# The start and the output stores of a three-stage fp32 kernel: w_out loads behind the last y store, unit 0 in the output banks, six output buffers

## The chip, the cores and the metric

One core of a Trainium2 chip runs the whole program. The metric is the device time of one execution in microseconds (us); 1 KB is 1024 bytes here. Engines are named as in the profile: PE (matmul), PEld (its weight loads), DVE, ACT, POOL, and SP, whose queue issues every DMA of this kernel.

## The reference, cut to what is computed

```python
x   = attn(q, k, v)            # 4 batches x 8 heads x 576 positions x 64: banded + pooled softmax
x   = x.transpose(0, 2, 1, 3).reshape(2304, 512)
a   = x @ w1; b = x @ w2       # 512 -> 1024
y   = (a * b @ w3) @ w_out     # 1024 -> 1024 -> 512
h   = y @ w_in                 # 512 -> 2048          (moe2)
out = (h * sigmoid(h)) @ w_out # 2048 -> 512, [2304, 512] fp32
```

## The kernel before

Every product is built from two fp32r parts of each operand (a high part and the remainder) in three passes, `PASSES`, so a result tile takes three matmuls for each 128 rows of the contraction.

**Stage one** (to about 454 us of the span) is attention, the first products (`ab_group`, tiles `ab`) and, for half a batch at a time, `y_group`: tile `y` is summed in a PSUM bank, ACT copies it to one of two `yo` buffers, and an SP DMA stores it to the DRAM tensor `ydram`. Weights of the last stage are decoded on the way and stored to the DRAM tensors `wsd` (w_in) and `wod` (w_out).

**The last stage** computes moe2 from `ydram`. Tokens are taken in three groups `t` of 768 and w_in in eight parts `p`; a **unit** `u = 8t + p` is one of the 24 combinations. `h_unit(u)` makes seven products `h_0` to `h_6` (six matmuls of 128x384 each, one round of a two-by-two block scheme that saves one product in eight). ACT copies `h_0` to `p1` (tile `p`), DVE combines each later product with what it has (tiles `u2`, `u4`, `u3`) into `cf` (ready after `h_4`) and `cg` (ready after `h_6`). `silu` then runs a sigmoid on ACT (tile `sg`), a multiplication on DVE, a cast on DVE to the high part of `g`, and a subtraction on POOL for the low part of `g`; the last three are `rest()`. `after(k, fn)` puts `fn` behind the k-th next product.

The outputs of a unit are summed one unit later: `out_block` adds three matmuls of 128x512 to one of six banks `o_0` to `o_5`; `run_out(2)` after each product but the first runs two of them. So a unit on PE is: `h_0`, `h_1`, two blocks, `h_2`, two blocks, and so on to `h_6`. Unit 0 has no blocks to run. After the last part of a token group the six sums are copied (ACT and DVE in turn) to a ring of `os` buffers and stored to `out`, two DMAs each.

**Banks.** PSUM has eight banks: a ring of two, `S` (`s_tile`), which the products `h` share; two `T`, which hold `o_0` and `o_1`; four `mm`, which hold `o_2` to `o_5` and, in stage one, `ab` and `y`. A product waits until the bank of the product two before it has been read.

**DMA.** `wc_load(u + 2)` at the end of `h_unit(u)` loads a unit's w_in parts, `wca` (768 KB) and `wcb` (1024 KB), from `wsd` into buffers that unit u frees. `wo_load(p)` loads 1024 KB of w_out (`wo`) from `wod`; `wo_load(0)` stands ahead of the stage, `wo_load(u + 1)` at the start of `h_unit(u)` for u below 7. `y_load(t)` loads `yr` (two DMAs of 768 KB) from `ydram`; POOL then makes four differences (`y_mix`, tile `t`, in units 2 to 5 of a group), ACT and DVE or POOL split them into `yc`.

**Order.** In the last stage PE, DVE, ACT and POOL run in source order (`manual_schedule`). SP isn't in that list: a scheduler puts its DMAs where it takes them to be ready. On each queue an instruction that waits holds all behind it.

Of the kernel before, what the change touches and what calls it, by code (L numbers as in the profile page):

```python
# [8 lines left out]
F32 = mybir.dt.float32  # L9
# [5 lines left out]
NB, NHP, S, P = 4, 4, 576, 128  # L15
# [20 lines left out]
def tile_model(ctx: ExitStack, tc: tile.TileContext, qk, vw, vr, w12, w3t, wo, wb, out):  # L36
    nc = tc.nc
    wide = wo.dtype != F32

    def pool(stack, name, side, space=None, bufs=1):  # L40
        kw = {} if space is None else {"space": space}
        return stack.enter_context(
            tc.tile_pool(name=name, bufs=bufs, side=side, reuse_waits="tile", **kw)
        )
# [11 lines left out]
    ydram = tc.dram_tile([4, P, NTOK], F32, name="ydram")  # L56
# [3 lines left out]
    def mm_tile(name):  # L60
        return ps.tile([P, 512], F32, tag="mm", name=name, bufs=4)
# [4 lines left out]
    def s_tile(name):  # L66
        return ps.tile([P, 512], F32, tag="S", name=name, bufs=2)
# [461 lines left out]
    def mark(ins):  # L529
        anchor[ins.ins.engine] = ins.ins  # L530
# [38 lines left out]
        C[b, h, m] = c  # L569

    y_ps = {}

    def y_group(b, h, ec, part):
        N = TOK[h]
        if part == 0:
            y_ps[ec] = mm_tile(f"y{b}_{h}_{ec}")
        acc = y_ps[ec]
        for kf in range(4 * part, 4 * part + 4):
            c = C[b, h, kf]
            for n, (i, j) in enumerate(PASSES):  # L580
                nc.tensor.matmul(  # L581
                    acc[:, :N], lhsT=WP[kf // 2][:, i, kf % 2, ec * P:(ec + 1) * P],
                    rhs=c[:, j, :],
                    start=(kf == 0 and n == 0), stop=(kf == 7 and n == 2),
                )
            if ec == 3:
                C.pop((b, h, kf))
        if part == 1:
            yo = cpool.tile([P, TOK[0]], F32, tag="yo", name=f"yo{b}_{h}_{ec}")[:, :N]
            mark(nc.scalar.copy(yo, acc[:, :N]))  # L590
            t0 = b * S + OFF[h]
            nc.sync.dma_start(ydram[ec, :, t0:t0 + N], yo)

    slots, kinds = [], []

# [15 lines left out]
    for part in range(2):  # L611
        for ec in range(4):
            slots.append(lambda ec=ec, part=part: y_group(NB - 1, 1, ec, part))
            kinds.append(None)
# [147 lines left out]
    def y_high(t, i):  # L762
        name = CH[i][0]
        d = yp[0].tile([P, 2, 2, NH], F32R, tag="c_" + name, name=f"yc{t}_{i}")
        nc.scalar.copy(d[:, 0], Y[t][name])
        YC[t, i] = d

    def y_rest(t, i, alone=False):
        d = YC[t, i]
        e = nc.vector if i % 2 or alone else nc.gpsimd  # L770
        e.tensor_tensor(
            out=d[:, 1], in0=Y[t][CH[i][0]], in1=d[:, 0].bitcast(F32), op=ALU.subtract
        )
# [15 lines left out]
    def wo_load(p):  # L789
        t = wpool.tile([P, 2, 2, 512], F32R, tag="wA" if p < 4 else "wC", name=f"wo{p}")  # L790
        nc.sync.dma_start(t.rearrange("p l f n -> p (l f n)").bitcast(F32), wod[p])
        WO[p] = t
# [47 lines left out]
    s_c.close()  # L840
    s_x.close()
    b2 = pool(ctx, "b2", "right", bufs=2)
    wo_load(0)

    todo = []

# [2 lines left out]
    def out_block(u, half, j):  # L849
        t, p = divmod(u, 8)  # L850
        if p == 0 and half == 0:
            OUT[t, j] = ps.tile(
                [P, 512], F32, tag="T" if j < 2 else "mm", name=f"o{t}_{j}",
                bufs=2 if j < 2 else 4,
            )
        acc = OUT[t, j]
        g, w = G[u, half], WO[p]
        for n, (a, b) in enumerate(PASSES):
            nc.tensor.matmul(  # L859
                acc, lhsT=g[:, a, j * P:(j + 1) * P], rhs=w[:, b, half, :],  # L860
                start=(p == 0 and half == 0 and n == 0), stop=(p == 7 and half == 1 and n == 2),
            )
        if p == 7 and half == 1:
            if t < NT - 1:
                o = b2.tile([P, 512], F32, tag="o", name=f"os{t}_{j}", bufs=3)
            else:
                if not last:
                    last.append(yp[0].tile([P, 6, 512], F32, tag="raw", name="last"))
                o = last[0][:, j]
            if j % 2:  # L870
                nc.vector.tensor_copy(o, acc)
            else:
                nc.scalar.copy(o, acc)
            for k in range(2):
                r0 = 64 * ORDER[(t * 2 * NH + j * P) // 64 + k]
                nc.sync.dma_start(out[r0:r0 + 64, :], o[64 * k:64 * k + 64, :])

    def run_out(n):
        for _ in range(min(n, len(todo))):
            out_block(*todo.pop(0))  # L880

    def temp(tag, u, bufs=1, width=NH):
        return b2.tile([P, width], F32, tag=tag, name=f"{tag}{u}", bufs=bufs)
# [4 lines left out]
    def after(k, fn):  # L888
        later.setdefault(n_chain[0] + k, []).append(fn)

    def next_chain():
        n_chain[0] += 1
        for fn in later.pop(n_chain[0], []):
            fn()

    def silu(u, half, c):
        sg = temp("sg", f"{u}_{half}", 2, 2 * NH)
        nc.scalar.activation(sg, c, AF.Sigmoid)  # L898
        g = b2.tile([P, 2, 2 * NH], F32R, tag="g", name=f"g{u}_{half}", bufs=5)
        G[u, half] = g  # L900

        def rest():
            nc.vector.tensor_tensor(out=sg, in0=c, in1=sg, op=ALU.mult)
            nc.vector.tensor_copy(g[:, 0], sg)  # L904
            e = nc.vector if u == NUN - 1 else nc.gpsimd
            e.tensor_tensor(  # L906
                out=g[:, 1], in0=sg, in1=g[:, 0].bitcast(F32), op=ALU.subtract
            )

        if half == 0 and u:  # L910
            rest()
        else:
            after(2 - half, rest)

    def h_unit(u):
        t, p = divmod(u, 8)
        wc = WC.pop(u)
        k = {}
        if u < 7:
            wo_load(u + 1)  # L920

        def tt(out_, in0, in1, op=ALU.add):
            nc.vector.tensor_tensor(out=out_, in0=in0, in1=in1, op=op)  # L923

        cf = temp("c", f"f{u}", 2, 2 * NH)
        cg = None
        for i, (name, w, c) in enumerate(CH):
            acc_full = s_tile(f"h{u}_{i}")
            acc = acc_full[:, :NH]
            y = YC[t, i]  # L930
            n = 0
            for kt in range(2):
                for (a, b) in PASSES:
                    nc.tensor.matmul(  # L934
                        acc, lhsT=wc[w][:, a, c, kt * P:(kt + 1) * P], rhs=y[:, b, kt, :],
                        start=(n == 0), stop=(n == 5),
                    )
                    n += 1
            if i == 0:
                k["p1"] = temp("p1", u)  # L940
                nc.scalar.copy(k["p1"], acc)  # L941
            elif i == 1:
                tt(cf[:, :NH], acc, k["p1"])
            elif i == 2:
                k["u2"] = temp("u2", u)
                tt(k["u2"], acc, k["p1"])
            elif i == 3:
                k["u4"] = temp("u4", u)
                tt(k["u4"], acc, k["u2"])
            elif i == 4:  # L950
                tt(cf[:, NH:], acc, k["u4"])
            elif i == 5:
                cg = temp("c", f"g{u}", 2, 2 * NH)
                k["u3"] = temp("u3", u)
                tt(k["u3"], acc, k["u2"])
                tt(cg[:, NH:], acc, k["u4"])
            else:
                tt(cg[:, :NH], k["u3"], acc, ALU.subtract)
            next_chain()
            if i == 4:  # L960
                silu(u, 0, cf)
            elif i == 6:
                silu(u, 1, cg)
            if p == 7 and t + 1 < NT:
                after(1, lambda i=i: y_high(t + 1, i))
                after(3, lambda i=i: y_rest(t + 1, i))
            if 2 <= p < 6 and i == 5 and t + 1 < NT:
                y_mix(t + 1, p - 2)
            run_out(2 if i else 0)
        wc_load(u + 2)  # L970
        if p == 1 and t + 1 < NT:
            y_load(t + 1)

    E = mybir.EngineType
    with tc.manual_schedule(engines={E.PE, E.DVE, E.Activation, E.Pool}):
        for u in range(NUN):
            h_unit(u)
            assert not todo
            todo.extend((u, half, j) for half in range(2) for j in range(6))
        for _ in range(3):  # L980
            next_chain()
        assert not later
        run_out(12)
# [56 lines left out]
```

## Time and profile before

| | |
|---|---|
| time, median of 3 runs | 884.74 us (883.40 to 886.43) |
| the profiled execution | 884.52 us, its span 882.7 us |
| PE busy | 846.1 us, 96% of the span |
| DVE, ACT, POOL busy | 533.8, 300.5, 277.5 us |
| mean granted TensorE clock | 0.988 of full speed |
| DMA over the span | 149.17 MB, mean 169 GB/s |

The span runs from the first to the last instruction; the time of an execution is 1.8 us longer. The ends of matmuls are modelled, so neighbouring PE rows can overlap by some tenths of a microsecond.

### The profile page before, as it was taken

Reading aid. Unit: us, or ns where it says so; the run is one execution under the profiler, and the core shown is the slowest. Engines: PE = TensorE matmul, PEld = TensorE weight load, DVE = VectorE, ACT = ScalarE, POOL = GpSimd, SP = SyncE. Lnnn points to the kernel's source line nnn. Section 1 sums busy time; section 2 is a strip of 40 time slices with the busy share of each in tenths; the row PEclk is TensorE's granted clock in tenths of the full one; section 3 lists DMA queues with packets and bytes.
Section 4 is the critical chain, followed back from the end, with each engine's and each line's share of the span. In section 5 each row is a group of like instructions: output and inputs, shape, how many; then the busy total and the mean of one; then the engine's idle time right before and its main releaser. Section 6 shows DMA issues by size and latency. Waiting matters only on the chain.

```text
span 882.7 us, 17438 instructions
## 1 busy us (share of the span) xinstructions
PE 846.1 (96%) x7104; PEld 745.7 (84%) x7104; DVE 533.8 (60%) x857; ACT 300.5 (34%) x866; POOL 277.5 (31%) x220
## 2 busy tenths in 40 slices
PE   3999999999999999999999799999999999999996
PEld 2544598999999999999999698989889899899995
DVE  5899989577475848447955334445544446543434
ACT  5665755454454544433322101114111122211101
POOL 2000154344442535231325123325323235221220
PEclk9999998999999999999999899999999999999999
DMA  9945735464545463406984824324743252642403
GB/s 325 341 136 164 236 121 186 145 238 162 181 164 197 158 213 114 169 27 236 336 337 183 337 91 124 127 85 166 212 135 129 84 167 84 182 140 85 164 3 72
DMA packets 39729, 149.17 MB, mean 169 GB/s; under 512 B 4448, under 2 KB 11616, under 8 KB 33504
## 3 DMA queue, kind: packets, MB, share of 16 engines
q1 hardware_dynamic: 39648, 148.05, 49.3%
q8 instruction: 56, 0.92, 0.4%
q14 instruction: 25, 0.20, 0.1%
HBM read 115.52 MB, written 32.51 MB: 168 GB/s over the span
## 4 chain that ended last, share of the span: by engine, by line
PE 83%; DVE 8%; DMA 3%; ACT 2%; issue 2%; SPq 0%; POOL 0%; ACTq 0%; DVEq 0%
PE o L859 21%; PE ab L541 20%; PE h L934 19%; PE y L581 10%; PE wp L451 5%; PE ol L371 2%; PE sd L279 2%; DMA ydram<-yo 2%; PE tl L347 2%; PE s L328 1%; PE od L313 1%; DMA out<-os 1%; PE td L296 1%; DVE dec L175 1%; DMA lent<-wo 1%
## 5 line engine op out<-in xcount | busy, mean ns | idle before, releaser
L859 PE MATMUL o<-wo,g 128*128 128x512 f32 x864 | 221.7, 393 | 2.0 <-POOL g L906 2.0
L859 PEld LDWEIGHTS o<-wo,g 128*128 128x128 f32 x864 | 160.6, 188 | 27.5 <-POOL g L906 2.3
L906 POOL TENSOR_TENSOR g<-sg,g 128x768 fp32r<-128x768 f32 x46 | 85.5, 1859 | 259.0 <-DVE g L904 249.7
L934 PE MATMUL h<-yc,wcb 128*128 128x384 f32 x576 | 119.0, 343 | 5.8 <-ACT p L941 5.8
L934 PEld LDWEIGHTS h<-yc,wcb 128*128 128x128 f32 x576 | 105.5, 192 | 14.6 <-ACT p L941 6.9
L541 PE MATMUL ab<-x,w_wB 128*128 128x320 f32 (+1 forms) x768 | 111.0, 299 | 0.6 <-DVE cf L555 0.6
L541 PE MATMUL ab<-x,w_wA 128*128 128x320 f32 (+1 forms) x768 | 108.9, 299 | 0.6 <-DVE w_wA L192 0.6
L581 PE MATMUL y<-c,w_wC 128*128 128x320 f32 (+1 forms) x768 | 109.3, 298 | 0.0
L541 PEld LDWEIGHTS ab<-x,w_wB 128*128 128x128 f32 x768 | 103.8, 190 | 2.1 <-issue 1.0
L541 PEld LDWEIGHTS ab<-x,w_wA 128*128 128x128 f32 x768 | 103.6, 191 | 1.9 <-DVE w_wA L192 0.9
L566 POOL TENSOR_TENSOR c<-cf,c 128x320 fp32r<-128x320 f32 (+1 forms) x64 | 72.1, 1127 | 101.0 <-DVE c L565 77.7
L581 PEld LDWEIGHTS y<-c,w_wC 128*128 128x128 f32 x768 | 102.6, 188 | 1.2 <-issue 1.0
L898 ACT ACTIVATE sg<-cf 128x768 f32<-128x768 f32 x24 | 20.3, 847 | 186.9 <-DVE cf L923 186.9
L934 PE MATMUL h<-yc,wca 128*128 128x384 f32 x432 | 83.4, 336 | 0.1
L934 PEld LDWEIGHTS h<-yc,wca 128*128 128x128 f32 x432 | 76.5, 188 | 4.2 <-DVE cg L923 0.4
L451 PE MATMUL wp<-w_wo,w_w 128*128 128x512 f32 x128 | 61.9, 629 | 1.3 <-DVE w_w L179 1.2
L238 POOL TENSOR_TENSOR vr<-vr 72x512 f32<-72x512 f32 x12 | 19.2, 1596 | 120.8 <-DMA vr<-vr 120.8
L555 DVE TENSOR_TENSOR cf<-ab,af 128x320 f32<-128x320 f32 (+1 forms) x64 | 28.8, 451 | 45.9 <-PE ab L541 36.5
L923 DVE TENSOR_TENSOR u<-h,u 128x384 f32<-128x384 f32 x48 | 26.6, 554 | 39.8 <-PE h L934 39.6
L898 ACT ACTIVATE sg<-cg 128x768 f32<-128x768 f32 x24 | 20.3, 847 | 87.7 <-DVE cg L923 87.7
L252 ACT ACTIVATE band<-band,sm 128x38 f32<-128x38 f32 x144 | 44.9, 316 | 8.4 <-DVE sm L248 7.4
L451 PEld LDWEIGHTS wp<-w_wo,w_w 128*128 128x128 f32 x128 | 24.2, 199 | 27.9 <-issue 24.1
(120 smaller groups left out, 1060.6 us busy)
## 6 DMA issues: line engine op xcount, KB each, us to landing
wcb<-wsd SPq DMA_DIRECT2D x24, 1024.0 KB
wca<-wsd SPq DMA_DIRECT2D x24, 768.0 KB
sw<-wb SPq DMA_DIRECT2D x32, 512.0 KB
qk<-qk SPq DMA_DIRECT2D x16, 579.0 KB
wsd<-res SPq DMA_DIRECT2D x8, 1024.0 KB
wod<-res SPq DMA_DIRECT2D x8, 1024.0 KB
wo<-wod SPq DMA_DIRECT2D x8, 1024.0 KB
st<-w SPq DMA_DIRECT2D x14, 512.0 KB
```

The source lines that it names most:

```text
L238: side().tensor_tensor(out=r[:, :, 0:2, :], in0=r[:, :, 0:2, :], in1=r[:, :, 2:4, :], op=ALU.add)
L252: nc.scalar.activation(E[:, j, :], src[:, j, :], AF.Exp, bias=nb[:, j:j + 1], scale=scale, accum_out=sv[:, j:j + 1],)
L451: nc.tensor.matmul(acc, lhsT=w3v[:, k, j * P:(j + 1) * P], rhs=wov[:, k, :], start=(gp == 0 and k == 0), stop=(gp == 3 and k == 1),)
L541: nc.tensor.matmul(acc[:, :N], lhsT=wv[:, i, w, kk, :], rhs=x[:, j, :], start=(n == 0), stop=(n == 11),)
L555: nc.vector.tensor_tensor(out=cf, in0=acc[:, :N], in1=C.pop("af"), op=ALU.mult)
L566: mark(nc.gpsimd.tensor_tensor(out=c[:, 1], in0=cf, in1=c[:, 0].bitcast(F32), op=ALU.subtract))
L581: nc.tensor.matmul(acc[:, :N], lhsT=WP[kf // 2][:, i, kf % 2, ec * P:(ec + 1) * P], rhs=c[:, j, :], start=(kf == 0 and n == 0), stop=(kf = ...
L859: nc.tensor.matmul(acc, lhsT=g[:, a, j * P:(j + 1) * P], rhs=w[:, b, half, :], start=(p == 0 and half == 0 and n == 0), stop=(p == 7 and h ...
L898: nc.scalar.activation(sg, c, AF.Sigmoid)
L906: e.tensor_tensor(out=g[:, 1], in0=sg, in1=g[:, 0].bitcast(F32), op=ALU.subtract)
L923: nc.vector.tensor_tensor(out=out_, in0=in0, in1=in1, op=op)
L934: nc.tensor.matmul(acc, lhsT=wc[w][:, a, c, kt * P:(kt + 1) * P], rhs=y[:, b, kt, :], start=(n == 0), stop=(n == 5),)
```

## The change

Five edits. `wo_load(0)` is recorded with `tc.issue_after` of the last y store, so its DMA stands behind that store in the program; unit 0 puts its first six products into the banks of the outputs (`mm` for `h_0` to `h_3`, `T` for `h_4` and `h_5`, `S` for `h_6`); unit 0's first `rest()` runs at once instead of two products later (for all other units nothing moves: `after(1, rest)` is what the second half had); the `os` ring has six buffers instead of three; and SP joins the engines that run in source order.

```diff
-            nc.sync.dma_start(ydram[ec, :, t0:t0 + N], yo)
+            last_y[:] = [nc.sync.dma_start(ydram[ec, :, t0:t0 + N], yo)]
...
-    wo_load(0)
+    with tc.issue_after(last_y[0].ins):
+        wo_load(0)
...
-                o = b2.tile([P, 512], F32, tag="o", name=f"os{t}_{j}", bufs=3)
+                o = b2.tile([P, 512], F32, tag="o", name=f"os{t}_{j}", bufs=6)
...
-        if half == 0 and u:
+        if half == 0:
             rest()
         else:
-            after(2 - half, rest)
+            after(1, rest)
...
-            acc_full = s_tile(f"h{u}_{i}")
+            bank = s_tile if u or i == 6 else mm_tile if i < 4 else t_tile
+            acc_full = bank(f"h{u}_{i}")
...
-    with tc.manual_schedule(engines={E.PE, E.DVE, E.Activation, E.Pool}):
+    with tc.manual_schedule(engines={E.PE, E.DVE, E.Activation, E.Pool, E.SP}):
```

On PE, where the last stage begins, the rows of before are these (`yc` the split inputs, the name in brackets whose signal a row waits for):

```order
L934 MATMUL h_2_6456<-yc_2_6157,wcb_5883 128x384 [waits DMAHW6_49,Activation_49]
L934 MATMUL h_2_6456<-yc_2_6157,wcb_5883 128x384 x5
L934 MATMUL h_3_6465<-yc_3_6111,wcb_5883 128x384 [waits DVE_49]
L934 MATMUL h_3_6465<-yc_3_6111,wcb_5883 128x384 x5
L934 MATMUL h_4_6474<-yc_4_6176,wcb_5883 128x384 [waits DVE_49]
...
L934 MATMUL h_0_6517<-yc_0_6077,wca_5903 128x384 [waits DMAHW0_49,DVE_49]
```

And of the changed kernel:

```order
L937 MATMUL h_2_6456<-yc_2_6157,wcb_5883 128x384 [waits DMAHW6_49,Activation_49]
L937 MATMUL h_2_6456<-yc_2_6157,wcb_5883 128x384 x5
L937 MATMUL h_3_6465<-yc_3_6111,wcb_5883 128x384 [waits Activation_49]
L937 MATMUL h_3_6465<-yc_3_6111,wcb_5883 128x384 x5
L937 MATMUL h_4_6474<-yc_4_6176,wcb_5883 128x384 [waits PE_49]
...
L937 MATMUL h_0_6517<-yc_0_6077,wca_5903 128x384 [waits DMAHW0_49]
L937 MATMUL h_0_6517<-yc_0_6077,wca_5903 128x384 x5
L937 MATMUL h_1_6529<-yc_1_6093,wca_5903 128x384 [waits DVE_49]
```

The products stand in the same order. In unit 0 the waits for DVE are gone; `h_0` to `h_3` wait for ACT, which must have copied the `y` tiles out of the same four banks. The first wait for DVE is now that of unit 1's `h_1`, whose bank is that of unit 0's `h_6`.

On SP, around the last y stores, before:

```order
L744 DMA yr_6637<-ydram 128x4x384
L791 DMA wo_6436<-wod 128x2048
L791 DMA wo_6514<-wod 128x2048
L744 DMA yr_6637<-ydram 128x4x384
L791 DMA wo_6640<-wod 128x2048
L592 DMA ydram<-yo_1_0_6378 128x256
L791 DMA wo_6759<-wod 128x2048
L592 DMA ydram<-yo_1_1_6393 128x256
L592 DMA ydram<-yo_1_2_6408 128x256
L791 DMA wo_6878<-wod 128x2048
L592 DMA ydram<-yo_1_3_6423 128x256
L791 DMA wo_6996<-wod 128x2048
```

And of the changed kernel:

```order
L593 DMA ydram<-yo_1_0_6378 128x256
L593 DMA ydram<-yo_1_1_6393 128x256
L593 DMA ydram<-yo_1_2_6408 128x256
L593 DMA ydram<-yo_1_3_6423 128x256
L792 DMA wo_6432<-wod 128x2048
L792 DMA wo_6436<-wod 128x2048
L782 DMA wca_6510<-wsd 128x1536
L785 DMA wcb_6511<-wsd 128x2048
L792 DMA wo_6514<-wod 128x2048
L782 DMA wca_6633<-wsd 128x1536
L785 DMA wcb_6634<-wsd 128x2048
L745 DMA yr_6637<-ydram 128x4x384 x2
```

No load of w_out is left ahead of the y stores. The first stands right behind the fourth store, the others one to a unit between the w_in loads, and the `yr` loads of the second token group have moved from ahead of the y stores to behind unit 3's w_in loads.

On SP, at the first output stores, before:

```order
L781 DMA wca_7359<-wsd 128x1536
L784 DMA wcb_7360<-wsd 128x2048
L744 DMA yr_7628<-ydram 128x4x384 x2
L876 DMA out<-os_0_7442 64x512 x2
L781 DMA wca_7503<-wsd 128x1536
L876 DMA out<-os_1_7449 64x512 x2
```

And of the changed kernel:

```order
L782 DMA wca_7359<-wsd 128x1536
L785 DMA wcb_7360<-wsd 128x2048
L878 DMA out<-os_0_7442 64x512 x2
L878 DMA out<-os_1_7449 64x512 x2
L878 DMA out<-os_2_7467 64x512 x2
L878 DMA out<-os_3_7474 64x512 x2
L878 DMA out<-os_4_7492 64x512 x2
L878 DMA out<-os_5_7499 64x512 x2
L782 DMA wca_7503<-wsd 128x1536
```

The w_in load that stood between the first and the second store now stands behind all twelve, and the `yr` loads of the third group stand two units later.

## Rows read from the trace of the kernel before

**Rows 1.** Windows: stretch, length, busy PE PEld DVE ACT POOL, clock, DMA share, GB/s.

```profile
488.00:510.00 22.00, 15.78 (x71) 14.39 (x70) 9.16 (x13) 3.30 (x6) 4.28 (x2) 0.84 0.79 300
520.00:614.00 94.00, 94.00 (x470) 84.78 (x469) 43.17 (x68) 17.80 (x25) 32.02 (x18) 1.00 0.36 119
```

**Rows 2.** Chain that ended last, 483 to 512 us: start, length, what.

```profile
485.51 7.75 DMA ydram<-yo
...
494.16 6.91 PE h L934 x24
...
508.16 1.07 PE h L934 x6
509.23 1.37 PE o L859 x6
```

**Rows 3.** Timeline, 455 to 515 us: start, length, engine, operation, idle before it.

```profile
476.79 0.52 SPq L791 DMA_DIRECT2D wo<-wod  x1
...
484.10 0.32 SPq L592 DMA_DIRECT2D ydram<-yo  x1
...
487.74 2.25 PE L934 MATMUL h<-yc,wca 128*128 128x384 f32 x12
490.53 0.37 ACT L590 COPY yo<-y 128x256 f32<-128x256 f32 x1 [5.05 <-DMA ydram<-yo]
...
493.63 0.48 ACT L941 COPY p<-h 128x384 f32<-128x384 f32 x1
...
494.14 0.56 DVE L923 TENSOR_TENSOR cf<-h,p 128x384 f32<-128x384 f32 x1 [16.32 <-ACT p L941]
...
504.23 2.45 POOL L906 TENSOR_TENSOR g<-sg,g 128x768 fp32r<-128x768 f32 x1 [25.53 <-DVE g L904]
```

**Rows 4.** Windows of four microseconds after PE's first idle time, columns as in rows 1.

```profile
492.00:496.00 4.00, 1.84 (x6) 1.84 (x7) 0.56 (x1) 0.75 (x2) 0.00 (x0) 0.59 0.89 310
496.00:500.00 4.00, 4.00 (x15) 4.00 (x14) 1.12 (x2) 0.00 (x0) 0.00 (x0) 0.56 1.01 423
...
504.00:508.00 4.00, 2.03 (x11) 1.44 (x10) 3.53 (x4) 0.06 (x1) 3.21 (x2) 1.00 0.77 298
```

**Rows 5.** Chain, last stage: the first two products of units 7, 8, 10, 16, 18.

```profile
598.67 2.08 PE h L934 x12
...
614.33 2.09 PE h L934 x12
...
646.58 2.09 PE h L934 x12
...
740.54 2.09 PE h L934 x12
...
773.02 2.08 PE h L934 x12
```

**Rows 6.** Timeline, 598 to 645 us, around the first output stores.

```profile
624.41 0.85 ACT L898 ACTIVATE sg<-cf 128x768 f32<-128x768 f32 x1 [7.73 <-DVE cf L923]
...
625.29 0.96 DVE L903 TENSOR_TENSOR sg<-cf,sg 128x768 f32<-128x768 f32 x1 [0.97 <-ACT sg L898]
625.75 1.22 SPq L876 DMA_DIRECT2D out<-os  x2
...
626.28 0.56 DVE L904 CAST g<-sg 128x768 fp32r<-128x768 f32 x1
...
629.40 0.69 DVE L871 COPY os<-o 128x512 f32<-128x512 f32 x1 [1.03 <-PE o L859]
...
633.11 0.59 ACT L873 COPY os<-o 128x512 f32<-128x512 f32 x1 [1.61 <-DMA out<-os]
```

**Rows 7.** Timeline, yr's loads of group 0, and the first differences of groups 0, 1.

```profile
454.44 0.97 SPq L744 DMA_DIRECT2D yr<-ydram  x2
...
463.39 2.45 POOL L760 TENSOR_TENSOR t<-yr 128x768 f32<-128x768 f32 x1 [7.64 <-DMA ydram<-yo]
...
534.77 1.85 POOL L760 TENSOR_TENSOR t<-yr 128x768 f32<-128x768 f32 x1
```

More of the change, by code (lines that the diff above doesn't have):

```diff
@@ L571, in tile_model @@
     y_ps = {}
+    last_y = []
     def y_group(b, h, ec, part):
```

## Prediction

> **What bounds the kernel now.** I read the windows by stage first. Between 520 and 614 us PE is busy for all 94.00 us while POOL has 32 and DVE 43 [rows 1]: there PE is the bound, and nothing is won by making another engine quicker. The one long stretch that differs is the start of the last stage, 488 to 510 us, where PE is busy for 15.78 of 22 us at a granted clock of 0.84 [rows 1]. The chain says what ended last there: a y store, 485.51 to 493.26 us, then 24 matmuls that take 6.91 us [rows 2]. The timeline shows how a store comes to hold PE. Loads of w_out are issued until 477.3 us; the first of the last four y stores is issued at 484.10, and the copy that needs its buffer back runs at 490.53, after 5.05 us of waiting for it. ACT is in order, so the copy of h_0 runs at 493.63, though h_0 and h_1 began at 487.74 and took 2.25 us; DVE, which needs that copy, starts at 494.14, and only then does a bank of the ring of two come free [rows 3]. PE, idle since 490, gets a low clock as well: 0.59 and 0.56 of full speed from 492 to 500 us, about the 1.2 GHz level, and 1.00 (2.4 GHz) later [rows 4].
>
> The second thing to see is the rhythm. Units 7 and 8 begin 15.66 us apart; from unit 8 to unit 10 it is 32.25 us, and from 16 to 18 it is 32.48, where two units of 15.66 would be 31.32 [rows 5]. These are the two places where outputs are stored: a DVE copy waits until 629.40 and an ACT copy until 633.11, the latter for a store out of the ring of three [rows 6]. So what can be won is at most the start plus 0.93 and 1.16 us.
>
> **Start of the stage, rebuilt for the changed kernel.** I take unit 1's h_2 as the mark; it stands at 508.16 in the chain [rows 2]. A product takes half of the 2.09 us of a pair, 1.045 [rows 5], and is readable some 0.17 us after the next could start (487.74 + 2.25 against 487.74 + 2.09) [rows 3, 5].
>
> The banks: h_0 to h_3 need the four copies of y. The y products end at the latest when h_0 starts, 487.74. The copies take 0.37 each [rows 3]. How long an undisturbed y store takes no row shows. Above, it is the 6.4 us from 484.10 to 490.53, with three megabytes of w_out and more ahead of it; below, nothing. The nearest row is the output store issued at 625.75 whose buffer is written again at 629.40 [rows 6], at most 3.65 us. I take 3.65: then the third copy runs at 487.8 and the fourth, whose store left at 485.5, at 489.2, the copy of h_0 ends at 490.0 and nothing waits, since h_3 isn't due before 490.9.
>
> PE then runs all seven products and unit 1's h_0 without a stop, to 487.74 + 8 x 1.045 = 496.1. Meanwhile h_4 is readable at 493.1; DVE combines it (0.56 [rows 3]) until 493.7; sigmoid 0.85, multiplication 0.96, cast 0.56 [rows 6], 496.2 with the gaps between them. This is the third edit: the multiplication and cast now stand ahead of DVE's last three combinations. They cost 1.5 us there, since those combinations, 0.55 each, end at 497.85 instead of about 496.3, and unit 1's h_1 needs the bank that the last of them frees. So PE idles for 1.75 us. What the early rest() buys is the low part of g: POOL, 2.45 us [rows 3], ends at 498.7. h_1 runs from 497.9, the two blocks follow at 498.95 (the second matmul, at 499.2, is the first to need the low part), take 1.37 [rows 2], and h_2 starts at 500.3. That is **7.8 us** earlier than 508.16. Bounds: with no idle at all 487.74 + 9 x 1.045 + 1.37 = 498.5, a gain of 9.6; the lower bounds are rivals below.
>
> What covers it: the blocks need the first load of w_out, which now leaves SP only behind the fourth y store, about 489.5. Two yr loads issued from 454.44, with megabytes ahead of them, had landed by 463.39, 8.95 us later [rows 7]; so long a time for 1024 KB in an almost empty queue would be 498.4, still before 498.95. It is hidden, by little in the worst case.
>
> **The other loads of w_out**, seven of 1024 KB, go from one burst to one per unit, between the w_in loads. A unit then moves 1024 + 768 + 1024 KB, 2.9 MB in 15.66 us or 184 GB/s, against 300 that were moved in the window at the start [rows 1]. Each is used more than a unit after it is issued. I cost them at nothing.
>
> **yr in source order.** The loads of groups 1 and 2 now stand behind two w_in loads that wait for PE; they are issued about 0.7 us before a unit that begins at T, with 1.8 MB ahead of their own 1.6. At 300 GB/s that is 11 us, T + 11. POOL's first difference runs at 534.77, which is T + 14.4 for unit 2 (598.67 less five units is 520.37) [rows 5, 7]. Hidden, by 3 us.
>
> **Output stores.** With six buffers no copy waits for a store: os_3 moves from 629.40 to about 628.4, os_4 from 633.11 to about 630.5, h_0's copy follows at 631.1, and PE's next h_2 isn't due before 633.3. The two transitions give back **0.93 + 1.16** us [rows 5]. Bounds: nothing (if the copies themselves, and not their buffers, hold ACT and DVE up), and all of it. I take all, as by these times each copy ends two microseconds before PE wants what stands behind it. The w_in load that now follows twelve stores leaves at about 634 instead of 627 and is needed at 645.
>
> **Sum.** 884.52 (profiled execution) - 7.8 - 0.93 - 1.16 = 874.6; the median of the runs is 0.22 above that execution, so **874.8 us**, 1.1% faster. With the bounds 9.6 and 7.0 for the start and 2.1 and 1 for the stores its own range is 873 to 877.
>
> **Rivals.**
> - *The clock falls anyway.* The 1.75 us of idle before unit 1's h_1 could pull PE to half speed. Against it: after the idle time of 4 us around 492 the clock was 0.59, but from 504 to 508, with PE busy for 2.03 of 4 us, it stayed at 1.00 [rows 4]. Eight microseconds at 0.56 to 0.59 would lose some 3.4: 878.2. Chance 0.09. (The Trainium skill, TensorE: Matmul & The Clock Gate, section on a second HAM failure mode, speaks for this rival: short idle times between groups of matmuls that cycle through PSUM banks can be enough for the clock to swing. The row above, of 2 us idle and full clock, does not show it.)
> - *Output stores give nothing back,* because copies and not buffers hold the ring: 876.9. Chance 0.05.
> - *The y stores are slow by themselves,* 6.4 us without any load ahead. Then h_0's copy stays at 493.6. The new banks let PE run to 496.1 all the same, but DVE's chain starts at 494.1, unit 1's h_1 at 500.4, h_2 at 502.8, and after 4.3 us of idle the low clock costs its 2.7 us (6.91 for what takes 4.18 [rows 2, 5]): a gain of 2.6, and 880.0 with the stores. Chance 0.04.
> - *It doesn't do what it says: PE waits for w_out instead.* If the first load landed at 508.7, the start gives nothing and 882.7 remains, no measurable change. That needs 19 us for one megabyte; 8.95 for more than two [rows 7] speaks against. Chance 0.04.
> - *Slower: the yr loads are late.* SP holds them behind waiting loads. POOL's difference may start up to about T + 21.3 without harm: behind it stand a difference and a low part of g, 1.85 each (the difference is in [rows 7]; the subtraction for g takes 1.85 too outside the start), which PE wants at T + 15.66 + 9.4. Beyond, each microsecond is one for PE, in groups 1 and 2. The gain is gone when they land at T + 26.2, it is slower by over 0.3% beyond T + 27.6; T + 28 would give 888.2. Estimated landing is T + 11. Chance 0.04.
>
> **How the numbers follow.** The forecast has the remaining 0.74. A change of 0.3% (2.7 us) is about what a measurement of this kernel can tell from none. Faster by more: forecast and the first three rivals, 0.92; within it: the fourth, 0.04; slower: the fifth, 0.04. The range 872.5 to 878.6 takes in the forecast with its bounds and the first two rivals.
>
> **What would show it.** Right: ACT copies h_0 before 490.1; no PE idle time over 0.5 us between the last y product and unit 1's h_1, then about 1.75 us released by DVE; clock 1.00 from 488 on; unit 1's h_2 near 500.3; units 8 to 10 and 16 to 18 at 31.3 us; no ACT or DVE copy released by an output store. Wrong: PE waiting for a wo load or for POOL at the first block; POOL's difference in units 2 or 10 released by a DMA; a granted clock near 0.6 after 496; the copies of y still released by their stores.

## The result and the profile after

The changed kernel takes 874.14 us (median of 4 runs, 871.77 to 874.99) against 884.07 for the kernel before (4 runs): an estimated ratio of 0.9877, 95% interval 0.9854 to 0.9901 (the two medians alone give 0.9888). The prediction was 874.8, in a range of 872.5 to 878.6. The medians differ by 9.93 us; the sum of the prediction was 9.89. The interval stands for 8.8 to 12.9 us, so the rows below are the sharper check.

Below, **M** is the start of unit 1's `h_2` in the chain less the start of unit 0's `h_0` in the timeline: 508.16 - 487.74 = 20.42 us before [rows 2, 3].

The windows of the changed kernel, columns as in rows 1:

```profile
488.00:492.00 4.00, 4.00 (x25) 4.00 (x24) 1.88 (x4) 0.85 (x1) 0.00 (x0) 1.00 0.99 406
492.00:496.00 4.00, 2.61 (x16) 2.29 (x15) 3.05 (x6) 1.21 (x2) 1.81 (x1) 1.00 0.93 354
496.00:500.00 4.00, 4.00 (x21) 3.49 (x20) 2.20 (x4) 0.00 (x0) 1.83 (x1) 1.00 0.97 375
...
488.00:510.00 22.00, 20.61 (x107) 18.76 (x106) 11.36 (x20) 3.75 (x5) 5.49 (x3) 1.00 0.72 261
520.00:614.00 94.00, 94.00 (x470) 84.77 (x469) 48.85 (x69) 18.53 (x26) 38.08 (x20) 1.00 0.46 163
```

PE is busy for 20.61 of the 22 us from 488 to 510 instead of 15.78, and the clock stays at 1.00 where it was 0.84, with 0.59 and 0.56 in its low part [rows 1, 4]. One idle time is left, between 492 and 496. From 520 to 614 PE was the bound and still is.

The timeline at the start of the last stage, with the engine's idle time and its releaser in brackets:

```profile
481.04 0.37 ACT L591 COPY yo<-y 128x256 f32<-128x256 f32 x1 [7.79 <-PE y L582]
482.40 0.37 ACT L591 COPY yo<-y 128x256 f32<-128x256 f32 x1 [0.99 <-PE y L582]
483.80 0.37 ACT L591 COPY yo<-y 128x256 f32<-128x256 f32 x1 [1.03 <-PE y L582]
484.92 2.25 PE L937 MATMUL h<-yc,wca 128*128 128x384 f32 x12
485.16 0.37 ACT L591 COPY yo<-y 128x256 f32<-128x256 f32 x1 [0.99 <-PE y L582]
486.00 0.85 SPq L792 DMA_DIRECT2D wo<-wod  x2
486.22 0.48 ACT L944 COPY p<-h 128x384 f32<-128x384 f32 x1 [0.68 <-PE h L937]
487.01 4.32 PE L937 MATMUL h<-yc,wcb 128*128 128x384 f32 x24
...
493.43 1.81 POOL L908 TENSOR_TENSOR g<-sg,g 128x768 fp32r<-128x768 f32 x1 [17.46 <-DVE g L906]
494.20 0.54 DVE L925 TENSOR_TENSOR cg<-u,h 128x384 f32<-128x384 f32 x1
494.80 1.34 PE L937 MATMUL h<-yc,wca 128*128 128x384 f32 x6 [1.39 <-DVE cg L925]
495.97 1.54 PE L861 MATMUL o<-wo,g 128*128 128x512 f32 x6
```

All four copies of y are now released by the product and none by a store; `h_0` is copied 1.3 us after it began, where it was 5.9 [rows 3]; the 24 matmuls of `h_2` to `h_5` take 4.32 us instead of 6.91 [rows 2]. PE stops once, for 1.39 us, until DVE's last combination has freed the bank of `h_6`.

The chain, with the first two products of units 8, 10, 16 and 18 as in rows 5:

```profile
494.80 1.34 PE h L937 x6
496.14 1.37 PE o L861 x6
497.51 1.06 PE h L937 x6
...
603.67 2.08 PE h L937 x12
...
634.99 2.08 PE h L937 x12
...
728.95 2.09 PE h L937 x12
...
760.27 2.09 PE h L937 x12
```

M is 497.51 - 484.92 = 12.59. Units 8 to 10 and 16 to 18 take 31.32 us each, two plain units exactly. So 7.83 + 0.93 + 1.16 = 9.92 us came from the two places. No DMA is left in the chain of the last stage.

The profiled execution itself took 871.77 us, 12.75 less than that of before. From the start of `h_0` to the end of the span it is 394.96 us before and 385.08 after, 9.88 less. The other 2.8 us came ahead of `h_0`, which began at 484.92 instead of 487.74. Up to the last store to `wod`, SP issues the same DMAs in the same order in both kernels, and 2.04 us of the difference are there by then. Before:

```profile
451.19 0.32 SPq L691 DMA_DIRECT2D wod<-res  x1
```

After:

```profile
449.15 0.32 SPq L692 DMA_DIRECT2D wod<-res  x1
```

These are not the change's. From that store to `h_0`, nine of the twelve traces of this case take 36.5 to 36.6 us, four with SP scheduled and five with SP in source order; that of the changed kernel takes 35.77, and why is open. In stage one the clock has low spells that differ from one execution to the next. The windows, and an ACT copy ahead of and behind the second spell, before:

```profile
100.00:104.00 4.00, 4.00 (x17) 1.93 (x14) 4.00 (x10) 2.19 (x13) 0.00 (x0) 0.57 0.62 189
148.00:152.00 4.00, 4.00 (x34) 3.94 (x31) 4.00 (x7) 2.24 (x7) 1.56 (x2) 0.50 0.71 203
152.00:156.00 4.00, 4.00 (x21) 4.00 (x21) 1.43 (x5) 0.86 (x4) 0.96 (x2) 0.65 0.73 292
```

```profile
144.64 0.53 ACT L351 COPY ET<-tl 102x256 f32<-102x256 f32 x2 [1.30 <-PE tl L347]
155.14 0.70 ACT L548 COPY af<-ab 128x320 f32<-128x320 f32 x2 [3.19 <-PE ab L541]
```

After:

```profile
96.00:100.00 4.00, 3.25 (x126) 3.09 (x124) 4.00 (x5) 1.15 (x1) 1.14 (x1) 0.87 0.84 283
100.00:104.00 4.00, 4.00 (x13) 1.87 (x12) 4.00 (x11) 2.59 (x15) 0.00 (x0) 0.50 0.56 165
104.00:108.00 4.00, 4.00 (x9) 1.77 (x8) 2.92 (x6) 1.84 (x11) 0.00 (x0) 0.78 0.82 261
```

```profile
145.68 0.53 ACT L351 COPY ET<-tl 102x256 f32<-102x256 f32 x2 [1.29 <-PE tl L347]
153.11 0.70 ACT L548 COPY af<-ab 128x320 f32<-128x320 f32 x2
```

The kernel before goes into the spell at 148 us 1.04 us ahead and comes out 2.03 behind: it lost 3.1 us there against the other execution, at a clock of 0.50 and 0.65. The missing share of full speed can't simply be added up, though: over stage one it is 3.4 us in the changed kernel and 1.7 in the run without the tie, and `h_0` began at the same time in both (484.92 and 484.93). That is why the comparison is made on medians and on M.

### The profile page after: what moved, and what is told of

The parts are those of the page before. It is cut to its first block, busy times and chain, and to the rows that moved or that the text cites. A ratio compares the mean times of both kernels' runs of the same rounds, so it can differ in the third digit from the quotient of the medians.

```text
span 870.0 us, 17423 instructions
## 1 busy us (share of the span) xinstructions
PE 839.1 (96%) x7104; PEld 739.6 (85%) x7104; DVE 532.2 (61%) x857; ACT 300.9 (35%) x866; POOL 276.4 (32%) x220
## 4 chain that ended last, share of the span: by engine, by line
PE 85%; DVE 8%; ACT 3%; issue 2%; DMA 1%; POOL 0%; SPq 0%; ACTq 0%; DVEq 0%
PE o L861 23%; PE h L937 20%; PE ab L541 18%; PE y L582 10%; PE wp L451 6%; PE ol L371 2%; PE sd L279 2%; PE tl L347 2%; PE od L313 1%; PE td L296 1%; ACT band L252 1%; PE s L328 1%; DMA ydram<-yo 1%; DMA lent<-wo 1%; DVE dec L175 1%
## 5 line engine op out<-in xcount | busy, mean ns | idle before, releaser
L937 PE MATMUL h<-yc,wcb 128*128 128x384 f32 x576 | 116.2, 337 | 0.0
L937 PEld LDWEIGHTS h<-yc,wcb 128*128 128x128 f32 x576 | 103.3, 188 | 7.7
L541 PE MATMUL ab<-x,w_wA 128*128 128x320 f32 (+1 forms) x768 | 106.4, 295 | 0.6 <-DVE w_wA L192 0.6
L541 PEld LDWEIGHTS ab<-x,w_wA 128*128 128x128 f32 x768 | 101.3, 188 | 1.9 <-DVE w_wA L192 0.8
```

The costliest lines, as they stand in the source:

```text
L541: nc.tensor.matmul(acc[:, :N], lhsT=wv[:, i, w, kk, :], rhs=x[:, j, :], start=(n == 0), stop=(n == 11),)
L937: nc.tensor.matmul(acc, lhsT=wc[w][:, a, c, kt * P:(kt + 1) * P], rhs=y[:, b, kt, :], start=(n == 0), stop=(n == 5),)
```

## The experiments

The theory: y stores stood in the queue behind loads that nobody needed yet, and source order on SP is what takes these away; banks, early multiplication and buffers are second lines. Rivals: the tie, or the banks, carry the gain. Ten kernels were run; each row's M is from its own trace, 31.3 is two plain units, and each ratio is to runs of the kernel before made beside that kernel (medians 883.47 to 884.51). M is one execution's: where the clock falls inside it, as in the rows with shared banks, queue only and w_out behind w_in, that is in it.

| kernel | M, us | units 8 to 10 | time, us | ratio to before (95%) |
|---|---|---|---|---|
| before | 20.42 | 32.25 | 884.07 | |
| changed | 12.59 | 31.32 | 874.14 | 0.9877 (0.9854 to 0.9901) |
| untied | 12.58 | 31.32 | 873.64 | 0.9882 (0.9853 to 0.9910) |
| SP scheduled, tied | 12.93 | 31.30 | 874.37 | 0.9887 (0.9855 to 0.9919) |
| shared banks | 14.72 | 31.32 | 874.40, one run | |
| late multiplication | 13.52 | 31.32 | 873.83, one run | |
| queue only | 13.92 | 31.32 | 875.22 | 0.9899 (0.9876 to 0.9922) |
| queue of before (no tie, SP scheduled) | 15.69 | 31.32 | 877.53 | 0.9923 (0.9893 to 0.9952) |
| tie only | 15.41 | 32.68 | 880.20 | 0.9949 (0.9926 to 0.9972) |
| unit 1's h_1 in an output bank | 11.83 | 31.32 | 872.89 | 0.9874 (0.9850 to 0.9898) |
| the same, low part by DVE | 11.37 | 31.32 | 871.96 | 0.9855 (0.9823 to 0.9887) |
| w_out behind w_in | 20.29 | 31.32 | 882.44, one run | |

**Without the tie.**

```diff
-    with tc.issue_after(last_y[0].ins):
-        wo_load(0)
+    wo_load(0)
```

> The changed kernel without the tie: the first load of w_out stands again ahead of the stage, SP still runs in source order, so only two loads of w_out (the first and the second) stand ahead of the last four y stores. Mark M: start of unit 1's h_2 less start of unit 0's h_0, 20.42 us before and 12.59 after. Theory (what held the copies was the burst of loads of w_out and yr in front of the stores, and source order alone breaks it up): M 12.6 +- 0.3, the copies of y not released by a store, time as after, 874. Rival (the tie is what frees the stores): third copy of y waits for its store, M over 15, time 877 to 881.

The theory's case: M 12.58, within a hundredth of the changed kernel's. With SP in source order only two loads of w_out are recorded ahead of the last y stores; the timeline has the second at 468.32 and the stores from 481.45. The tie adds nothing once the queue is in order.

**SP left to the scheduler, tie kept.**

```diff
-    with tc.manual_schedule(engines={E.PE, E.DVE, E.Activation, E.Pool, E.SP}):
+    with tc.manual_schedule(engines={E.PE, E.DVE, E.Activation, E.Pool}):
```

> The changed kernel with SP left to the scheduler: the first load of w_out stays behind the last y store, but the scheduler puts the yr loads and three other loads of w_out (for parts 4 to 6) between the y products' stores. Theory: the stores are late again, h_0's copy with them; new banks let PE run ahead, so M 14 to 18 instead of 12.6, low clock if PE then idles for 3 us or more; time 876 to 880. Output stores: six buffers, so units 8 to 10 and 16 to 18 take 31.3 us although a w_in load stands between the stores. Rival (tying the first load is what counts): M 12.6, time 874.

The queue did what the theory says, the time did not. In the timeline the copies wait for stores again:

```profile
488.00 0.37 ACT L591 COPY yo<-y 128x256 f32<-128x256 f32 x1 [1.30 <-DMA ydram<-yo]
491.88 0.37 ACT L591 COPY yo<-y 128x256 f32<-128x256 f32 x1 [3.50 <-DMA ydram<-yo]
492.14 0.49 ACT L944 COPY p<-h 128x384 f32<-128x384 f32 x1
```

`h_0`, begun at 488.95, is copied 3.2 us later instead of 1.3, and M is 12.93: 1.9 us of lateness cost 0.34. With a bank for each product PE goes on, and DVE, which takes 0.56 us for a product that PE makes in 1.045, has caught up by `h_4`. What is left is PE's own wait for the fourth copy of y, whose bank `h_3` needs:

```profile
492.30 3.10 PEld L937 LDWEIGHTS h<-yc,wcb 128*128 128x128 f32 x18 [0.38 <-ACT yo L591]
```

My estimate of 14 to 18 left that catching up out. M and time came out near where the rival had them (12.6 and 874), and beside the banks, the early multiplication and the buffers the tie does count: without it, in the run with the queue of before below, M is 15.69. By itself it isn't what counts: the run with the tie alone has M 15.41.

**Unit 0 in the ring of two again.**

```diff
-            bank = s_tile if u or i == 6 else mm_tile if i < 4 else t_tile
-            acc_full = bank(f"h{u}_{i}")
+            acc_full = s_tile(f"h{u}_{i}")
```

> The changed kernel with unit 0's products in the ring of two banks again. Theory (once h_0's copy is on time the ring is read fast enough; only unit 1's h_0 waits, for DVE's reads of h_5, which now come behind the early multiplication and cast): M 13.1, 0.5 more than after. Rival (the new banks are worth most of the gain): every product waits for DVE, M over 15.

M 14.72 lies between the two. The timeline and the windows have the reason:

```profile
494.82 3.91 PE L936 MATMUL h<-yc,wca 128*128 128x384 f32 x12 [1.97 <-DVE cg L925]
```

```profile
492.00:496.00 4.00, 2.03 (x9) 1.71 (x9) 2.91 (x5) 0.99 (x2) 1.83 (x1) 0.87 1.01 384
496.00:500.00 4.00, 4.00 (x17) 3.75 (x16) 2.08 (x3) 0.58 (x2) 1.85 (x1) 0.70 0.99 403
```

PE waits where expected, for DVE's last combinations, 1.97 us. Then the clock falls, and twelve matmuls take 3.91 us where they take 2.25 [rows 3]. Without these 1.66 us M would be 13.06, the expected 13.1. Unit 0's products do not wait: once `h_0`'s copy is on time, the ring of two is enough until unit 1.

**Unit 0's first multiplication and cast two products later.**

```diff
-        if half == 0:
+        if half == 0 and u:
             rest()
         else:
-            after(1, rest)
+            after(2 - half, rest)
```

> The changed kernel with unit 0's first multiplication and cast two products later again. Theory: DVE frees h_6's bank 1.5 us sooner, so unit 1's h_1 doesn't wait, but POOL's low part of g comes about 1 us later and the second matmul of the first block waits for it: M 12.8 to 13.3, PE's wait released by POOL and not by DVE. Rival (the early rest is worth microseconds, or nothing): M over 14, or 12.6 and less.

M 13.52, a little above the expected 13.3. PE's stop is now at the first block, 2.03 us, released by POOL:

```profile
498.13 1.43 PE L861 MATMUL o<-wo,g 128*128 128x512 f32 x5 [2.03 <-POOL g L908]
```

So the early `rest()` is worth 0.93 us, net of the 1.39 us for which it makes PE wait on DVE.

**The queue alone.** The kernel before, with SP added to the engines that run in source order and nothing else.

```diff
-    with tc.manual_schedule(engines={E.PE, E.DVE, E.Activation, E.Pool}):
+    with tc.manual_schedule(engines={E.PE, E.DVE, E.Activation, E.Pool, E.SP}):
```

> The kernel before with one edit of the five: SP runs in source order. No tie, the products of unit 0 in the ring of two, its multiplication and cast late, three output buffers. Theory (the queue's order holds up both places, so this edit alone brings nearly all): copies of y not released by stores, M 13.0 to 13.5 (up to 15 if an idle time of 2 us before the blocks pulls the clock down, as it did with shared banks), units 8 to 10 and 16 to 18 at 31.3 to 31.5 us with three buffers, time 874.5 to 877, ratio 0.990. Rival (banks and buffers are needed): M over 15 without a low clock, transitions at 32 us, time over 878.

875.22 us, 9.3 under its runs of before (884.51), from one edit of five. M is 499.74 - 485.82 = 13.92 (two rows of the timeline, one of the chain):

```profile
485.82 2.25 PE L934 MATMUL h<-yc,wca 128*128 128x384 f32 x12
497.94 1.81 PE L859 MATMUL o<-wo,g 128*128 128x512 f32 x5 [1.98 <-POOL g L906]
```

```profile
499.74 1.92 PE h L934 x6
```

A low clock (0.85 and 0.73 in the windows from 496 to 504 us) is in it: the first `o` group after the wait of 1.98 us for POOL takes 1.81 us for five matmuls, 1.43 in the run with late multiplication. It costs more after the mark, where `h_2` takes 2.12 instead of 1.21. Units 8 to 10 take 31.32 us with three buffers: stores that leave at once free them in time.

**The queue of before (no tie, SP scheduled), the three other edits kept.**

```diff
-    with tc.issue_after(last_y[0].ins):
-        wo_load(0)
+    wo_load(0)
...
-    with tc.manual_schedule(engines={E.PE, E.DVE, E.Activation, E.Pool, E.SP}):
+    with tc.manual_schedule(engines={E.PE, E.DVE, E.Activation, E.Pool}):
```

> The changed kernel with SP left to the scheduler and no tie: the queue of before, all loads of w_out and yr around the y stores, but the new banks, the early multiplication and cast and six output buffers. Unit 0's h_0 is copied about 5.9 us after its start as before, instead of 1.3. By the chain of the prediction (copy, four combinations, sigmoid, multiplication, cast, three combinations, h_1, two blocks) M is 15 to 16, and up to 17.5 with a low clock; time 877 to 879. Rival, after the run with SP left to the scheduler and the tie (a copy 3.2 us late cost 0.3): the banks swallow it all, M 12.6 to 13, time 874.5.

Time and M as expected. The timeline shows the new wait that the banks bring: PE needs the banks of y, so it waits for the copies of y itself.

```profile
488.17 2.25 PE L936 MATMUL h<-yc,wca 128*128 128x384 f32 x12
491.44 1.32 PE L936 MATMUL h<-yc,wcb 128*128 128x384 f32 x6 [1.02 <-ACT yo L591]
494.28 3.42 PE L936 MATMUL h<-yc,wcb 128*128 128x384 f32 x18 [1.52 <-ACT yo L591]
```

Idle in pieces of 1.0, 1.5 and 1.4 us, the clock stayed at 1.00. Units 8 to 10 took 31.32 us with the scheduler's order of the stores: six buffers alone also do it.

**The tie alone,** on the kernel before (only the first two hunks of the change).

> The kernel before with the tie alone: the first load of w_out behind the last y store, SP still scheduled (three other loads of w_out and both yr loads stand between the stores, as in the run with SP left to the scheduler), products in the ring of two, late multiplication and cast, three output buffers. h_0's copy should run 3.2 us after h_0's start, as in that run; without new banks h_2 waits for it, 1.6 us, on top of the 13.5 to 13.9 of the runs with late multiplication: M 15 to 15.6, up to 17 with a low clock. Units 8 to 10 and 16 to 18 at 32.2 and 32.5 us as before. Time 879 to 881. Rival (the tie alone frees the stores): M 13.5, time under 878.

M 15.41 and 880.2 us, both as expected; 32.68 and 32.50 us at the output stores, with `DMA out<-os` in the chain at both. By M the tie alone brings 5.0 of the 7.83 us at the start and nothing at the output stores. It moves one load, and the scheduler then puts three others and both yr loads between the y stores.

**The first two loads of w_out behind unit 2's w_in loads.**

```diff
         wc_load(u + 2)
+        if u == 0:
+            wo_load(0)
+        if u < 7:
+            wo_load(u + 1)
```

(and the two earlier calls removed)

> The changed kernel with the first two loads of w_out behind unit 2's w_in loads, which wait until unit 0's last product is done; measures the cover of the load that the tie makes late. The load leaves at 7.9 us after the stage's start instead of about 1.1 and has 1.8 MB ahead of it. Theory: it lands at 13 to 16 us, PE waits for it at the first block, M 14.5 to 18, and a wait of 2 us or more. Rival (hidden still): M 12.6.

```profile
494.66 1.11 SPq L792 DMA_DIRECT2D wo<-wod  x2
```

```profile
504.18 2.93 PE L859 MATMUL o<-wo,g 128*128 128x512 f32 x6 [6.15 <-DMA wo<-wod]
```

A wait of 6.15 us, released by the load, M 20.29: worse than expected. The load took 9.5 us from its issue, behind 1.8 MB; my 13 to 16 us after the start were 17.4. The clock was 0.50 from 500 to 508 us, so the first block group took 2.93 us instead of 1.54. So in the changed kernel the load is hidden because it leaves 1.1 us after `h_0`'s start; this one wait, with the low clock after it, eats all of the start's gain.

**Two versions beyond the change.** In the first, unit 1's `h_1` takes the output bank that `h_0`'s copy freed; in the second, DVE also makes unit 0's first low part of g.

```diff
-            bank = s_tile if u or i == 6 else mm_tile if i < 4 else t_tile
+            bank = mm_tile if (u, i) == (1, 1) else s_tile if u or i == 6 else mm_tile if i < 4 else t_tile
...
-            e = nc.vector if u == NUN - 1 else nc.gpsimd
+            e = nc.vector if u == NUN - 1 or (u, half) == (0, 0) else nc.gpsimd
```

> The changed kernel with unit 1's h_1 in an output bank as well (the one that h_0's copy freed), so that it doesn't wait for DVE's last combination. Theory: PE's wait of 1.4 us goes; the second matmul of the first block then waits some 0.8 us for POOL's low part; M 11.4 to 11.7, time about 1 us under the changed kernel, 873. Rival (POOL's low part is the next limit, at the same time): M 12.4, no change.

> The run with unit 1's h_1 in an output bank, and unit 0's first low part of g made by DVE (0.96 us) instead of POOL (1.8). If POOL's low part is what is left at the first block: no PE idle time over 0.4 us in the first two units, M 10.9 to 11.2, time 872. Rival (DVE's later combinations, 0.96 us later, then hold unit 1's h_2): M stays at 11.8.

M 11.83, then 11.37: 0.76 and 1.22 us under the changed kernel, 0.1 and 0.2 above the ranges that I expected. In the first PE still waits 0.64 us for POOL; in the second 0.19 us for DVE's combinations, which now come later. The medians, 872.89 and 871.96, have the same order, but their intervals overlap that of the change: M tells these apart, the time does not.

## Why the prediction was right

- **What bounded the start.** Right, and shown from both sides: the queue's order alone takes M from 20.42 to 13.92, and with the queue of before the three other edits (banks, early multiplication, buffers) leave it at 15.69.
- **The term of 7.8 us.** It was 7.83 (M 12.56 against 12.59), with small errors that cancel, to 0.03 by luck: DVE freed the bank at 9.8 us after the start, not 10.1, and PE idled 1.39 us, not 1.75; the first product after the wait took 1.34 us instead of 1.045; POOL's low part took 1.81 us, not 2.45, and held nothing up.
- **The y stores.** I took 3.65 us as an upper bound. The third copy came 2.4 us after the end of the first and did not wait for its store, so a store in an empty queue takes at most 2.4. (The Trainium skill, DMA: Bandwidth & Descriptors, section on the anatomy of one DMA, has about 2 us fixed plus the bytes at 436 GB/s for a DMA of the gpsimd path, for these 128 KB an estimate of 2.3; these stores are issued from SP, and of them the trace shows the 2.4 as an upper bound only.)
- **The early multiplication.** The prediction priced its cost at 1.5 us and took its use for granted; undone, M rises by 0.93. Right in sign.
- **0.93 and 1.16 us at the output stores.** Both came back in full. The prediction put them down to six buffers, though it had the store order too: either alone is enough.
- **Costed at nothing.** No block waited for w_out, and no difference on POOL for a yr load (the first, below, has no idle time before it). Right, though the experiment with the late load shows that the cover of w_out is the queue's order and not slack in general.

```profile
524.25 1.86 POOL L761 TENSOR_TENSOR t<-yr 128x768 f32<-128x768 f32 x1
```

- **Rivals.** The low clock did not come in the changed kernel (idle 1.39 us); its mechanism is real, see below. The late stores were priced at M 15.06 plus 2.7 for the clock: with the old queue, which makes them as late (6.5 us from the first store to the third copy), M was 15.69, and the clock did not fall. The rival's step that PE runs to 496.1 all the same was wrong: `h_2` and `h_3` need banks of y and waited 1.0 and 1.5 us for the copies of y, so the idle time came in pieces. That the pieces are why the clock stayed up isn't shown.

What the prediction did not say is which edit does it. By the runs, SP in source order by itself brings about nine tenths (6.50 of the 7.83 us of M, and all of the 0.93 and 1.16 at the output stores). It isn't the only way: the four other edits without it come within 0.34 us of M (12.93), with a median of 874.37. Beside the source order the tie brings nothing, the early multiplication 0.93 us of M, the banks 0.5 us, or 2.1 with the low clock that followed in their one run, and the buffers nothing at units 8 to 10. With the queue of before, banks, early multiplication and buffers together bring M from 20.42 to 15.69 and units 8 to 10 from 32.25 to 31.32; no run has banks or early multiplication alone there.

## What to carry to other kernels

Where an engine that copies results waits for a store, look in the queue for loads ahead of it that nobody needs yet, and put the queue in the order of need before adding buffers or banks; these then guard what is left. Rebuild the stretch in time with measured durations, up to a mark in the trace: the mark shows a difference of half a microsecond that the time of a run, which moves by 3 us with the clock, does not. Undo edits in pairs, since two remedies for one wait each look worthless, or each look like all of it.

## What the hardware showed

- **An idle time of 2 us may or may not pull the clock down.** At the start of the last stage it fell after 1.97 us (shared banks, to 0.70 in the next window) and after 1.98 us (queue only), not after 2.03 (late multiplication), 1.96 (tie only) nor 1.97 in the kernel before, where it was 1.00 from 504 to 508 [rows 4] and on to 512; and not after 1.0 to 1.6 us in any run. A fall cost 1.7 us in one case. (The Trainium skill, TensorE: Matmul & The Clock Gate, section on a second HAM failure mode, says that frequent short idle times between groups can do this; at 2 us the traces agree in two runs of five.) The row of before:

```profile
506.74 1.42 PE L859 MATMUL o<-wo,g 128*128 128x512 f32 x5 [1.97 <-POOL g L906]
```

- **Low clock in stage one comes in some executions and not in others, at the same places of the code.** Of the twelve traces all have a spell between 96 and 108 us, seven one between 148 and 156, five one between 12 and 32. The one at 148 us cost the kernel before 3.1 us. Of the four runs of the changed kernel, those of 871.77 and 873.56 us have a mean clock of 0.994, those of 874.72 and 874.99 us 0.984 and 0.985.
- **One megabyte behind 1.8 others took 9.5 us from its issue.** All 2.9 MB at the 300 GB/s of [rows 1] would be an estimate of 9.6.
